# Four accumulators in the first down matmul of a pooled-attention and gated-MLP kernel on one Trainium2 core

## The chip, the cores and the metric

The kernel runs on one core of one Trainium2 chip. The metric is the device time in microseconds (us); three runs of the kernel before gave a median of 284.59 us (284.47 to 284.63). Engines are named as in the profile: PE is TensorE's matmul, PEld its weight load, DVE is VectorE, ACT is ScalarE, POOL is GpSimd, SP is SyncE, which here only issues DMA.

## The reference

Eight batches with eight heads of 576 rows of 64 are attended to keys and values that are averaged over groups of eight rows, so each head has only 72 keys. The result, read as 4608 tokens of 512, goes through an MLP whose activation is `h * cos(h)`.

```python
k_p = k.reshape(B, H, Sp, 8, D).mean(axis=3)       # Sp = 72
v_p = v.reshape(B, H, Sp, 8, D).mean(axis=3)
scores = scale * np.matmul(q, k_p.transpose(0, 1, 3, 2))
attn = softmax(scores)
x = np.matmul(attn, v_p).transpose(0, 2, 1, 3).reshape(4608, 512)
h = x @ w_in                                       # 512 x 2048
out = (h * np.cos(h)) @ w_out                      # 2048 x 512
```

## The kernel before

The tokens are cut into nine tiles of 512 (`t` = 0 to 8). For each tile an up stage multiplies by `w_in` (`up_mm`, L354), takes the cosine on ACT (L364) and the product on DVE (L368), which gives `g_sb`; a down stage then multiplies `g_sb` by `w_out`. While the down stage of tile t runs, the attention of batch b = t + 1 is computed in between, since the next up stage needs it. The order of the work on each engine is the order of the program text; the queues are not reordered.

From tile 1 on the down stage uses seven products in place of eight, for which sums of the blocks of `w_out` are needed. `put_weights(i, nc.vector, ks)` makes them on DVE (L388): for each half `i` four sums named 1, 3, 2 and 4, of which 2 needs 3 and 4 needs 2. Half 0 reads the blocks `w_out_sb[0]` and `[2]`, half 1 the blocks `[1]` and `[3]`. The blocks are loaded in the order 0, 2, 1, 3.

Tile 0 is the only one whose down stage is the plain product, 64 matmuls of 128x128 weights by 512 columns (`down_mm`, L371): four row blocks of 128 tokens (`ms`) times sixteen steps of the contraction (`fc`), four to a block of `w_out` (`cg`). Before, it works on two row blocks at a time, accumulated in `obanks[0]` and `obanks[1]`, and takes for each pair all four blocks of `w_out` in the order 0, 2, 1, 3. `down_out` copies a finished row block to SBUF on DVE (L376) and stores it from SP (L380).

The list `fill` puts the attention of batch 1 between these matmuls: `(n, f)` runs `f` ahead of matmul `n`. `S_(j, bank)` is the scores of unit `j`: four matmuls on 64 rows (L234) and an Exp on ACT (L241). `V_(j, bank)` is the values: four matmuls (L269), two Ln (L275) and an Exp (L276) on ACT, and two multiplies on DVE (L280), which read the same PSUM and write `xT`, the input of the next up stage. With `later` as the last argument the two multiplies are kept back, and `later.pop()()` issues them. `REST` is the last 64 rows of batch 0. `pool_v_mm` pools the values of batch 1 by matmul (L186, with its copy on DVE L188).

PSUM is laid out as three pairs of banks, `banks[0]` to `banks[2]`, and two single ones, `obanks`. The first up stage after tile 0 begins by writing `banks[0]`, then `banks[2]`, then `banks[1]`, then `obanks`.

GpSimd pools the keys and values of batches 2 to 7 (`pool_first`, L157; `pool_rest`, L163 to L169), starting when the keys of batch 2 have landed, during tile 0's down stage. At the very start the keys of batch 0 are pooled by matmul and copied to `kk` by `put_kk`, four copies for each pair of heads (L151).

Of the kernel before, what the change touches and what calls it, by code (L numbers as in the profile page):

```python
# [9 lines left out]
FP32 = mybir.dt.float32  # L10
# [10 lines left out]
def kernel(  # L21
# [9 lines left out]
    nc = tc.nc  # L31
    B, H, S, D = q.shape
    Sp = S // POOL
    d_model = H * D
# [112 lines left out]
    def put_kk(b, ps, pj0, pj1, copy):  # L147
        for a in range(2):
            for r in range(2):
                j = key_slot(b, 2 * pj0 + a, r)  # L150
                copy(out=kk[b % 2][half[r], j:j + pj1 - pj0, 0:Sp], in_=ps[half[a]])  # L151

    def pool_first(b, which):

# [16 lines left out]
    def pool_k_mm(b, bank, pj0, pj1):  # L171

        kb = staged["k", b]
        ps = bank[:, 0:(pj1 - pj0) * Sp].rearrange("p (j n) -> p j n", n=Sp)
        for pj in range(pj0, pj1):
            for t in range(ROW):
                for rows in half:
                    nc.tensor.matmul(ps[rows, pj - pj0, :], lhsT=kb[rows, pj, t, :], rhs=groups[rows, t, :],  # L178
                                     start=(t == 0), stop=(t == ROW - 1))
        return lambda copy: put_kk(b, ps, pj0, pj1, copy)  # L180
# [42 lines left out]
    def scores(b, u, pair):  # L223
        scores_mm(b, u, pair)
        scores_exp(b, u, pair)
# [145 lines left out]
        nc.tensor.matmul(o, lhsT=g_sb[:, fc, ms * 128:(ms + 1) * 128],  # L371
                         rhs=w_out_sb[fc // 4][:, fc % 4, :], start=(fc == 0), stop=(fc == FFCH - 1))

    def down_out(t, ms, ps):
        o = msb.tile([128, 2, d_model], FP32, name="o_two", tag="o_two", bufs=2)[:, 0]
        nc.vector.tensor_copy(out=o, in_=ps)  # L376
        rows_of = out.rearrange("(b p t) m -> b t p m", b=B, t=ROW)
        for i, rows in enumerate(half):
            b_, pos = divmod((t * TILE + ms * 128) // 64 + i, ROW)
            nc.sync.dma_start(out=rows_of[b_, ORDER[pos]], in_=o[rows])  # L380
# [151 lines left out]
    early_inverses += ["p1_sb", "v_sb", "q_sb"] * 3  # L532

    warm_up(10, obanks[0])
    pool_k_mm(0, obanks[1], 0, 2)(vec)
    warm_up(2, banks[1][:, 0, :])
    puts = q_transpose_mm(0, banks[2][:, 0, :], 0, 5), q_transpose_mm(0, obanks[0], 5, 9)
    puts[0](vec)
# [24 lines left out]
    for t in range(NT):  # L563
        b = t + 1
        if t > 0:

            for fp in up_order(t)[0:2]:
                up_mm(t, fp, 0, 2)
        for n, fp in enumerate(up_order(t)):
            up_mm(t, fp, 2 if n < 2 else 0)  # L570
            between = ()
            if t == 0:
                if fp == 4:
                    puts = pool_k_mm(1, obanks[0], 0, 2), pool_k_mm(1, obanks[1], 2, 4)
                elif fp in (5, 6):
                    g0 = 9 * (fp - 5)
                    puts = q_transpose_mm(1, obanks[0], g0, g0 + 5), q_transpose_mm(1, obanks[1], g0 + 5, g0 + 9)
                if fp in (4, 5, 6):
                    puts[0](vec)
                    between = ((puts[1], act),)  # L580
            up_g(t, fp, between)

            late = {5: (1,), 6: (3,)} if t == 1 else {4: (1, 2), 5: (3,)}
            sums = {} if t == 0 else late if b < B else {3: (1, 2), 4: (3,), 5: (4,)}
            put_gs(*[(i, 0) for i in sums.get(n, ())])
            if 0 < t and b < B:
                if n == 0:
                    q_transpose(b)
                    k_transpose(b)
                elif n == 2:  # L590
                    pool_rest(b, "v")
                    if b + 1 < B:
                        nc.gpsimd.tensor_copy(out=gate, in_=kk[b % 2][0:1, H - 1, 0:1])
                        load_q(b + 1)
                        load_kv(b + 1, "v", v)
            if n == 2:
                while stores:
                    stores.pop(0)()
        mms = [(ms, fc) for ms in range(4) for fc in range(FFCH)]
        if t == 0:  # L600
            mms = [(ms, fc) for hm in range(2) for cg in (0, 2, 1, 3) for ms in range(2 * hm, 2 * hm + 2)
                   for fc in range(4 * cg, 4 * cg + 4)]


        def S_(n, bank):
            return lambda: scores(b, us[n], banks[bank])

        later = []

        def V_(n, bank, wait=None):  # L610
            return lambda: values(b, us[n], banks[bank], wait)

        fill = []
        if t < B:
            exp_tables()
            fill = [(1, lambda: scores(t, REST, banks[2])), (16, lambda: values(t, REST, banks[1]))]
        if t == 0:
            fill = [(2, lambda: scores(t, REST, banks[1])), (2, S_(0, 0)), (8, lambda: pool_v_mm(1, banks[2])),
                    (8, lambda: values(t, REST, banks[1])),
                    (8, lambda: put_weights(0, nc.vector, (3, 2))), (8, S_(1, 0)), (8, V_(0, 2)),  # L620
                    (18, S_(2, 1)), (18, lambda: put_weights(0, nc.vector, (4,))),
                    (18, lambda: put_weights(1, nc.vector, (1,))), (21, V_(1, 0, later)), (26, S_(3, 2)), (32, lambda: later.pop()()),
                    (32, V_(2, 1)), (40, V_(3, 0))]
        if t == FIRST:
            early_inverses.clear()
        if t < FIRST:
            fi = 0
            for n, (ms, fc) in enumerate(mms):
                while fi < len(fill) and fill[fi][0] <= n:
                    fill[fi][1]()  # L630
                    fi += 1
                down_mm(obanks[ms % 2], ms, fc)
                if fc == FFCH - 1:
                    down_out(t, ms, obanks[ms % 2])
                if n == 4:
                    put_weights(0, nc.vector, (1,))
                elif n == 36:
                    put_weights(1, nc.vector, (3,))
            put_weights(1, nc.vector, (2, 4))
        else:  # L640
            products, reads = down_products(t)

            def product(i, j=0, k=2 * HF):
                for mm in products[i][j:k]:
                    mm()

            later = []

            u0, u1, u2, u3 = [(b, CHUNKS[i], banks[j]) for i, j in enumerate((2, 1, 0, 1))]
            ur = (t, REST, banks[2])  # L650

            def scores_of(*parts):
                for part in parts:
                    scores_mm(*part)
                for part in parts:
                    scores_exp(*part)

            def muls():
                while later:
                    later.pop(0)()  # L660

            steady, rest = b < B, t < B
            if rest:
                exp_tables()

            product(0, 0, 12)
            product(1, 0, 4)
            product(0, 12)
            reads[0]()
            if steady:  # L670
                scores_of(u0, u1, u2)
            elif rest:
                scores_of(ur)
            product(1, 4)
            if t == 1:
                put_g(2, 0)
            put_gs((1, 1), (2, 1))
            if not steady:
                reads[1]()
            put_gs((3, 1), (4, 1))  # L680
            if steady:
                reads[1]()
                put_g(4, 0)
                values_rows(*u0)
            product(2)
            reads[2]()
            if steady:
                values_rows(*u1)
                values_rows(*u2)
            product(3)  # L690
            reads[3]()
            muls()
            product(4)
            reads[4]()
            muls()
            if steady:
                scores_of(ur, u3)

            product(5, 0, 6)
            if rest:  # L700
                values(*ur, later)
            product(5, 6, 12)
            muls()
            if steady:
                values_rows(*u3)
            product(5, 12)
            reads[5]()
            muls()
            product(6)
            reads[6]()  # L710
        if t < B:
            sin_tables()
        if b + 1 < B:
            if t == 0:
                load_kv(b + 1, "k", k)
                load_q(b + 1)
                load_kv(b + 1, "v", v)
            else:

                nc.gpsimd.tensor_copy(out=gate, in_=g4[0:1, 0, 0:1])  # L720
            pool_first(b + 1, "k")
            if t != 1 and b + 2 < B:
                load_kv(b + 2, "k", k)
            pool_rest(b + 1, "k")
            if t == 1:
                load_kv(b + 2, "k", k)
            pool_first(b + 1, "v")
# [28 lines left out]
```

## Time and profile before

| | |
|---|---|
| median of three runs | 284.59 us |
| span of the profiled execution | 282.8 us |
| tile 0, first down matmul starts | 33.45 us |
| tile 1, first up matmul starts | 53.05 us |
| GpSimd's first pooling of keys starts | 46.37 us |
| down matmul L371, mean of one | 379 ns |
| weight sums L388 at 39.76, 40.48, 43.08 and 43.69 us | 0.68 to 0.69 us each |
| weight sums L388 at 49.00, 53.86 and 55.56 us | 1.30, 1.67 and 1.64 us |
| issue to landing of a block of w_out | 18.2 to 18.7 us |

All times are counted from the start of the span. [...]

### The profile page before, as it was taken

How to read it: one execution, taken by the hardware profiler on the slowest of the kernel's cores; microseconds unless marked ns; L12 is line 12 of the kernel's file. 1: busy time of each engine (PE TensorE's matmuls, PEld its weight loads, DVE VectorE, ACT ScalarE, POOL GpSimd, SP SyncE). 2: the span in 40 equal slices, each digit the busy share in tenths (PEclk: the TensorE clock that was granted, in tenths of full speed). 3: DMA queues.
4: the chain of work that ended last, by engine and by line, in shares of the span. 5: the costliest groups of instructions: out<-in, count | busy, mean ns of one | idle time of the engine just before them, and what ended most of it. 6: DMA issues, size and time to landing. Idle time of an engine off the chain costs nothing.

```text
span 282.8 us, 5887 instructions
## 1 busy us (share of the span) xinstructions
PE 275.2 (97%) x2378; PEld 185.4 (66%) x2378; DVE 212.6 (75%) x313; ACT 167.3 (59%) x199; POOL 132.1 (47%) x146
## 2 busy tenths in 40 slices
PE   7899999999999999999999999999999999999994
PEld 3555554456875687568756975688558855875683
DVE  5448769889946995699568966896689669846972
ACT  3787798368357735774567556655666555436600
POOL 8542114995599259934993389539910000000000
PEclk9999999999999999999999999999999999999999
DMA  7999999795739798997688959882660260005015
GB/s 153 201 206 209 212 207 216 132 190 84 118 60 163 125 215 140 136 175 155 101 148 146 189 80 163 156 174 52 125 148 3 58 148 19 2 21 127 2 37 112
DMA packets 56202, 36.13 MB, mean 128 GB/s; under 512 B 35440, under 2 KB 51312, under 8 KB 56176
## 3 DMA queue, kind: packets, MB, share of 16 engines
q0 software_dynamic: 18208, 18.07, 40.8%
q1 hardware_dynamic: 37328, 17.18, 29.7%
q10 hardware_dynamic: 640, 0.52, 0.8%
q8 instruction: 18, 0.29, 0.4%
q14 instruction: 8, 0.07, 0.1%
HBM read 36.70 MB, written 9.44 MB: 163 GB/s over the span
## 4 chain that ended last, share of the span: by engine, by line
PE 92%; ACT 3%; DMA 2%; DVE 1%; issue 1%; POOL 0%; POOLq 0%; DVEq 0%
PE bank L354 39%; PE obank L432 33%; PE obank L354 5%; PE obank L371 4%; PE bank L234 3%; DMA q_b<-in_q_dram 2%; PE bank L296 2%; PE bank L432 2%; ACT ex L241 1%; PE bank L269 1%; PE obank L178 0%; DVE g_sb L368 0%; PE obank L215 0%; PE bank L186 0%; ACT cos L364 0%
## 5 line engine op out<-in xcount | busy, mean ns | idle before, releaser
L354 PE MATMUL bank<-xT,w_in_sb 128*128 128x512 bf16 x512 | 113.8, 379 | 0.1
L364 ACT ACTIVATE cos<-bank,half_pi 128x1024 f32<-128x1024 f32 x64 | 70.4, 1115 | 55.9 <-PE bank L354 55.9
L354 PEld LDWEIGHTS <-w_in_sb 128*128 128x128 bf16 x576 | 64.9, 113 | 57.4 <-issue 0.3
L368 DVE TENSOR_TENSOR g_sb<-bank,cos 128x1024 bf16<-128x1024 f32 x64 | 77.0, 1221 | 30.5 <-ACT cos L364 30.3
L157 POOL TENSOR_TENSOR half_sums<-kv_st 72x512 f32<-72x512 bf16 x48 | 54.4, 1158 | 8.4 <-DMA kv_st<-in_k_dram 8.0
L241 ACT ACTIVATE ex<-bank 72x1024 bf16<-72x1024 f32 (+1 forms) x40 | 35.0, 931 | 30.0 <-PE bank L234 30.0
L432 PEld LDWEIGHTS <-g 128*128 128x128 bf16 x512 | 47.8, 98 | 5.8
L432 PE MATMUL obank<-w,g 128*128 128x256 bf16 x368 | 42.6, 272 | 0.0
L432 PEld LDWEIGHTS <-g_sb 128*128 128x128 bf16 x384 | 37.0, 98 | 6.4
L163 POOL TENSOR_TENSOR half_sums<-half_sums 72x512 f32<-72x512 f32 x24 | 30.0, 1273 | 0.0
L432 PE MATMUL obank<-w_out_sb,g_sb 128*128 128x256 bf16 x240 | 28.9, 273 | 0.0
L398 DVE TENSOR_TENSOR g<-g_sb 128x1024 bf16<-128x1024 bf16 x32 | 21.9, 685 | 0.3
L720 POOL COPY gate<-g 1x1 bf16<-1x1 bf16 x5 | 0.9, 180 | 37.9 <-DVE inv_rows L299 37.9
L280 DVE TENSOR_TENSOR xT<-bank,inv 64x256 bf16<-64x256 f32 x14 | 5.9, 422 | 15.4 <-ACT inv L276 15.4
L301 DVE TENSOR_TENSOR x_rows<-bank,inv_rows 128x512 bf16<-128x512 f32 x24 | 16.6, 692 | 0.8
L432 PE MATMUL obank<-w_out_sb,g 128*128 128x256 bf16 x112 | 15.6, 273 | 0.0
L432 PE MATMUL obank<-w,g_sb 128*128 128x256 bf16 x128 | 15.3, 272 | 0.0
L371 PE MATMUL obank<-w_out_sb,g_sb 128*128 128x512 bf16 x64 | 15.2, 379 | 0.0
L354 PE MATMUL obank<-xT,w_in_sb 128*128 128x512 bf16 x64 | 15.1, 379 | 0.0
L234 PE MATMUL bank<-qT,kk 64*72 64x128 bf16 (+2 forms) x288 | 12.3, 221 | 0.1
L332 ACT ACT_TABLE_LOAD x9 | 11.5, 1283 | 0.9 <-PEq L740 0.7
L234 PEld LDWEIGHTS <-kk 64*72 64x72 bf16 x288 | 8.7, 110 | 5.1 <-issue 3.4
(99 smaller groups left out, 270.0 us busy)
## 6 DMA issues: line engine op xcount, KB each, us to landing
out_dram<-o_two SPq DMA_DIRECT2D x64, 128.0 KB, 2.4
kv_st<-in_v_dram POOLq DMA_DIRECT2D x8, 576.0 KB, 12.3
kv_st<-in_k_dram POOLq DMA_DIRECT2D x7, 576.0 KB, 8.1
q_b<-in_q_dram POOLq DMA_DIRECT2D x6, 576.0 KB, 7.6
w_in_sb<-in_moe_w_in_dram POOLq DMA_DIRECT2D x4, 512.0 KB, 13.5
w_out_sb<-in_moe_w_out_dram POOLq DMA_DIRECT2D x4, 512.0 KB, 18.6
q_b<-in_q_dram POOLq DMA_DIRECT2D x4, 288.0 KB, 12.3
g_sb<-in_k_dram SPq DMA_DIRECT2D x1, 576.0 KB, 3.4
```

The costliest lines, as they stand in the source:

```text
L157: nc.gpsimd.tensor_tensor(out=s[:, h:h + 2], in0=x[:, h:h + 2, 0:4, :], in1=x[:, h:h + 2, 4:8, :], op=ADD)
L163: add(out=s[:, h:h + 4, 0:2, :], in0=s[:, h:h + 4, 0:2, :], in1=s[:, h:h + 4, 2:4, :], op=ADD)
L234: nc.tensor.matmul(pair[:Sp, bank, c:c + n].rearrange("p (g n) -> p g n", n=64), lhsT=kk[b % 2][half[r], key_slot(b, h0 + i, r), 0:Sp], rh ...
L241: nc.scalar.activation(out=ex[:, 0:nh * n].rearrange("p (a n) -> p a n", a=2), in_=pair[:Sp, :, 0:nh * n // 2], func=ACTF.Exp, scale=scale ...
L301: nc.vector.tensor_tensor(out=x[0:n].rearrange("p (j a d) -> p j a d", j=KCH, a=2), in0=ps[0:n, :, 0:2 * (D + 2)].rearrange("p j (a w) -> ...
L332: nc.scalar.preload_act_table_set("natural_log_exp_and_others")
L354: nc.tensor.matmul(h[j] if h is obanks else h[:, j, :], lhsT=w_in_sb[fc // 4][:, ki, fc % 4:512:4], rhs=xT[:, ki, t * TILE:(t + 1) * TILE] ...
L364: nc.scalar.activation(out=c, in_=ps, func=ACTF.Sin, bias=half_pi[:, :1])
L368: nc.vector.tensor_mul(out=o, in0=ps, in1=c)
L371: nc.tensor.matmul(o, lhsT=g_sb[:, fc, ms * 128:(ms + 1) * 128], rhs=w_out_sb[fc // 4][:, fc % 4, :], start=(fc == 0), stop=(fc == FFCH - 1))
L398: nc.vector.tensor_tensor(out=out[:, f0:f1], in0=x, in1=y, op=op)
L432: mms.append(lambda bank=bank, first=first, g=g, w=w, fc=fc, p=p: nc.tensor.matmul(bank[p], lhsT=g(fc, p), rhs=w(fc), start=(first and fc ...
```

## The change

The plain down stage of tile 0 gets four accumulators: the two `obanks` and the two halves of `banks[1]`. All four row blocks first use the blocks 0 and 2 of `w_out`, and after matmul 31 the blocks 1 and 3, in the row order 2, 3, 0, 1; so the blocks are used as they land. Row blocks 2 and 3 are copied out together, when the second of them is done. As `banks[1]` is taken from matmul 16 on, the attention's units are moved between `banks[0]` and `banks[2]` and to other places in the list, and the multiplies kept back are those of `V_3` in place of `V_1`. The sums 3 and 2 of half 1 are made ahead of matmul 34, before GpSimd's pooling; before, sum 3 came after matmul 36 and sum 2 at the end. The output tiles are allocated as two whole ones in place of four halves. And at the start half of the first pooled-key copies goes to ACT.

```diff
-                copy(out=kk[b % 2][half[r], j:j + pj1 - pj0, 0:Sp], in_=ps[half[a]])
+                (copy if callable(copy) else copy[a])(out=kk[b % 2][half[r], j:j + pj1 - pj0, 0:Sp], in_=ps[half[a]])
...
-    pool_k_mm(0, obanks[1], 0, 2)(vec)
+    pool_k_mm(0, obanks[1], 0, 2)((vec, act))
...
-            mms = [(ms, fc) for hm in range(2) for cg in (0, 2, 1, 3) for ms in range(2 * hm, 2 * hm + 2)
-                   for fc in range(4 * cg, 4 * cg + 4)]
-            fill = [(2, lambda: scores(t, REST, banks[1])), (2, S_(0, 0)), (8, lambda: pool_v_mm(1, banks[2])),
-                    (8, lambda: values(t, REST, banks[1])),
-                    (8, lambda: put_weights(0, nc.vector, (3, 2))), (8, S_(1, 0)), (8, V_(0, 2)),
-                    (18, S_(2, 1)), (18, lambda: put_weights(0, nc.vector, (4,))),
-                    (18, lambda: put_weights(1, nc.vector, (1,))), (21, V_(1, 0, later)), (26, S_(3, 2)), (32, lambda: later.pop()()),
-                    (32, V_(2, 1)), (40, V_(3, 0))]
...
-                down_mm(obanks[ms % 2], ms, fc)
-                if fc == FFCH - 1:
-                    down_out(t, ms, obanks[ms % 2])
-                if n == 4:
-                    put_weights(0, nc.vector, (1,))
-                elif n == 36:
-                    put_weights(1, nc.vector, (3,))
-            put_weights(1, nc.vector, (2, 4))
+            mms = [(ms, 4 * cg + f) for cgs, mss in (((0, 2), (0, 1)), ((0, 2), (2, 3)), ((1, 3), (2, 3, 0, 1)))
+                   for cg in cgs for ms in mss for f in range(4)]
+            acc = [*obanks, banks[1][:, 0, :], banks[1][:, 1, :]]
+            os = [msb.tile([128, 2, d_model], FP32, name="o_two", tag="o_two", bufs=2) for _ in range(2)]
+            fill = [(2, lambda: scores(t, REST, banks[1])), (2, S_(0, 0)),
+                    (4, lambda: put_weights(0, nc.vector, (1,))),
+                    (8, lambda: pool_v_mm(1, banks[2])), (8, lambda: values(t, REST, banks[1])),
+                    (8, lambda: put_weights(0, nc.vector, (3, 2))), (8, S_(1, 0)), (8, V_(0, 2)),
+                    (18, lambda: put_weights(0, nc.vector, (4,))), (20, lambda: put_weights(1, nc.vector, (1,))),
+                    (20, V_(1, 0)), (28, S_(2, 2)), (34, lambda: put_weights(1, nc.vector, (3, 2))), (35, S_(3, 0)), (36, V_(2, 2)),
+                    (44, V_(3, 0, later)), (57, lambda: later.pop()())]
...
+                down_mm(acc[ms], ms, fc)
+                if fc == FFCH - 1 and ms != 2:
+                    for m in (2, 3) if ms == 3 else (ms,):
+                        down_out(t, m, acc[m], os[m // 2][:, m % 2])
+            put_weights(1, nc.vector, (4,))
```

## The prediction before the run

> **What bounds the kernel now.** I read the page's busy shares first, then the chain that ended last in order of time, then the timelines of PE and of DVE from 40 us on, where the edited stage lies. The page:
>
> ```profile
> PE 275.2 (97%) x2378; PEld 185.4 (66%) x2378; DVE 212.6 (75%) x313; ACT 167.3 (59%) x199; POOL 132.1 (47%) x146
> PEclk9999999999999999999999999999999999999999
> ```
>
> TensorE is busy 97% at full clock, so a change can help only where PE stands still, and hurts wherever it makes PE stand still. Is there standing still in the first down stage (33.45 to 53.05 us)? The chain, in order of time (start, length, what):
>
> ```profile
> 38.70 2.16 PE obank L371 x10
> ...
> 45.66 1.73 PE obank L371 x8
> 47.38 0.04 issue
> 47.42 0.61 PE bank L269 x4
> 48.03 5.18 PE obank L371 x24
> 53.22 5.18 PE bank L354 x24
> 58.40 1.73 PE obank L354 x8
> 60.12 6.91 PE bank L354 x32
> ```
>
> From 38 us to the end nearly everything is PE, and from 48 us on no wait is left. So what the stage gains or loses goes one to one into the total. The PE timeline of the stage:
>
> ```profile
> 40.79 0.41 PE L234 MATMUL bank<-qT,kk 64*72 64x256 bf16 x4
> 41.13 0.82 PE L371 MATMUL obank<-w_out_sb,g_sb 128*128 128x512 bf16 x3
> 41.79 0.60 PE L269 MATMUL bank<-ex,vz 72*128 72x256 bf16 x4
> 42.23 1.24 PE L371 MATMUL obank<-w_out_sb,g_sb 128*128 128x512 bf16 x5
> 45.49 1.89 PE L371 MATMUL obank<-w_out_sb,g_sb 128*128 128x512 bf16 x8
> 47.42 0.61 PE L269 MATMUL bank<-ex,vz 72*128 72x256 bf16 x4
> ```
>
> A row's length holds the drain of its last matmul; starts give the pace: 24 matmuls in 5.18 us is 0.216 us each. The eight from 45.49 are issued by 47.22, and the next group starts at 47.42: 0.20 us of real waiting. Now DVE:
>
> ```profile
> 41.66 1.39 DVE L280 TENSOR_TENSOR xT<-bank,q_sb 64x512 bf16<-64x512 f32 x2 [0.48 <-ACT q_sb L276]
> 43.08 0.69 DVE L388 TENSOR_TENSOR w<-w_out_sb,w 128x1024 bf16<-128x1024 bf16 x1
> 43.69 0.68 DVE L388 TENSOR_TENSOR w<-w_out_sb 128x1024 bf16<-128x1024 bf16 x1
> 45.98 1.39 DVE L280 TENSOR_TENSOR xT<-bank,p_sb 64x512 bf16<-64x512 f32 x2
> 49.00 1.30 DVE L388 TENSOR_TENSOR w<-w_out_sb,w_out_sb 128x1024 bf16<-128x1024 bf16 x1
> 52.39 0.69 DVE L376 COPY o_two<-obank 128x512 f32<-128x512 f32 x1 [0.67 <-PE obank L371]
> 53.26 0.69 DVE L376 COPY o_two<-obank 128x512 f32<-128x512 f32 x1 [0.17 <-PE obank L371]
> 53.86 1.67 DVE L388 TENSOR_TENSOR w<-w,w_out_sb 128x1024 bf16<-128x1024 bf16 x1
> ```
>
> The pair of multiplies from 45.98 ends at 47.37; PE's group at 47.42 writes the same bank pair (banks[0]), so that wait is for them. Its first matmul writes only the first bank of the pair, which only the first multiply (done at about 46.67) reads, yet it waited for the second. **The wait is for the pair of banks as a whole.** Much hangs on this below.
>
> **What the Trainium skill says.** "PSUM — Partial Sum Buffer", PSUM bank collisions raise a hardware error: a bank must be guarded by bank and quadrant. That would let PE into one bank while DVE reads its neighbour; the 47.42 start shows the program waiting more coarsely. "SBUF — State Buffer", Who interferes with whom: a DVE instruction with two SBUF inputs contends with a GpSimd one that reads SBUF. The trace agrees: weight sums take 0.69 us before GpSimd's pooling starts (46.37) and 1.30 to 1.67 after. "TensorEngine Tiling (Array Packing)", Key Properties: changing the tiling mode drains TensorE. Trace: from the last of three L371 matmuls to L269 the step is 0.21 us, but a score group (64 rows) begins 0.31 us after the last L371 start and the next L371 0.34 us after the group, about 0.09 us lost each way. The change keeps the number of such switches.
>
> **The change part by part.** I number the 64 down matmuls n.
>
> Start-up: half of the first pooled-key copies moves to ACT. The four DVE copies run from 6.71 to 7.99, but the next chain piece waits for q's DMA to 7.65 and then for its transposes, and DVE takes up qT only at 8.19. ACT is idle from 5.4 to 8.4. Cost and gain: nothing, hidden by that DMA.
>
> n = 0 to 17: same order, same fills, so PE reaches n=8 at 38.54 as before. Blocks 1 and 3 of w_out move from n=16 and 24 to n=32 and 48. They were issued at 21.30 and 24.12 and take 18.6 us, so they land at 39.9 and 42.7 or a little earlier; n=16 ran at 40.27 and n=24 at 42.88. PE did not wait for them; the later use gains nothing.
>
> n = 18 to 34, PE: n=8 to 19 without a score group, 12 x 0.216, so V_1 (values, L269) at 41.13; 0.44 for it, n=20 at 41.57; eight more to 43.30; S_2 (scores, L234) at 43.39, n=28 at 43.73; n=34 at 45.04; ready for S_3 at about 45.35.
> DVE in the same time: V_0's multiplies end 43.05 as before; sum 4 of half 0 to 43.77, sum 1 of half 1 to 44.37 (both as before); then V_1's two multiplies, 1.39, 44.41 to 45.80. Their input is in time (ACT: V_1's two Ln from 41.77, 1.20, and Exp 0.63, done 43.6).
> S_3 writes banks[0], which V_1's multiplies read until 45.80, so it starts at 45.85. **New wait: 0.50 us.** In place of it the old 0.20 wait disappears.
>
> n = 35 to 63, PE: n=35 at 46.19, V_2 at 46.42, n=36 at 46.86, V_3 at 48.59, n=44 at 49.03, n=55 from 51.40 to 51.78, n=63 done issuing at 53.34 (0.30 later than 53.05).
> The two weight sums at n=34 go in DVE at 45.83 to 47.9 (0.69, then about 1.3 under pooling; 1.67 at worst) while V_2 waits for ACT anyway: after Exp of S_3 (46.30 to 47.30) its Ln and Exp end at 49.16, its multiplies at 50.57. That removes 1.3 + 1.67 us of slow sums, but DVE had 20.4 us busy in 25 there and PE never waited for them: no gain.
>
> The end: the outputs of row blocks 2 and 3 now lie in the two halves of banks[1] and are both copied after n=55; then come V_3's multiplies, held back until n=57. DVE is in order, so: copy 2, copy 3, multiply, multiply. If the copy of block 2 waits for the last write of the bank pair, which is how I read 47.42, it starts at 51.81; two copies 1.41, two multiplies 1.42: done 54.64. The next up stage begins with banks[0], which V_3's multiplies read: its first matmul at about 54.70 instead of 53.34. **New wait: 1.36 us.** Behind it in PE's queue stands the whole rest of the kernel. In the old kernel these multiplies were over at 51.72.
>
> Sum: 0.50 - 0.20 + 1.36 = 1.66 us, 284.59 + 1.66 = 286.2. Nothing later takes it back, since PE has no wait from 48 us on. DVE afterwards: copies of blocks 0 and 1 to 56.1, one slow sum to 57.8, and the first product of the up stage, at 57.13 before and 1.66 later now, is hardly touched. The stores of tile 0 come about 2 us later in SP's queue, ahead of the transposes that the scores at 69.14 need; these transposes were issued by 63.70, so over 3 us of slack remain.
>
> **The rivals.**
> Waits by bank, not by pair: the copy of block 2 starts after n=51 (50.95), block 3's at 51.81, multiplies end at 53.92; up starts at 53.98 (+0.93), or, if the first up matmuls need only the first multiply, only a second short wait of 0.2 remains (+0.5). 285.1 to 285.5. For it: the rule by bank and quadrant; against it: 47.42.
> No new waits (multiplies early enough, by an order of work that I misjudge): the 0.20 goes, 284.4, not slower. Against: three DVE durations added in program order.
> Faster by 0.2% would need 0.57 us. Such a sum is not there: all gaps of the stage beyond the mode switches are some 0.6 us, most of them ahead of n=8 where nothing changes. Only if the real reason for the block order, landing w_out blocks, bit in unprofiled runs could it come; the profiled run took 284.58, the median, so no. About 284.0.
> Worse: pooling also slows the weight sums and delays V_2's multiplies past 50.9: 286.6 or more.
>
> **How the numbers follow.** Pair-wise waits 0.74 (286.2, spread 285.9 to 286.6), by bank 0.12, no new waits 0.09, faster 0.05. Range 285.0 to 286.6. Slower by over 0.2% (285.16): 0.85, the by-bank case lying across the edge; same 0.10; faster 0.05.
>
> **What would show it.** In the new profile: a PE wait on DVE L280 of about 0.5 us before the score group near 45.8; two L376 copies back to back near 51.8 and then L280 twice; PE's first L354 of tile 1 near 54.7 with L280 as its releaser; from there on the old chain, shifted. Wrong would be a PE without gaps from 41 to 53, copies that start before n=55 has ended, or an up stage that starts before V_3's multiplies end.

## The result and the profile after

The changed kernel takes 286.59 us in the median of six runs (286.13 to 287.19) against 284.53 for six runs of the kernel before (the three runs above and three more): a ratio of 1.0078, 95% interval 1.0061 to 1.0094. It is slower by 2.06 us between the medians and by 2.2 us by the ratio, where 1.66 was forecast; on the 284.59 us from which the forecast started, the ratio makes 286.8. From the page of the changed kernel, the busy times and the shares of the chain that ended last:

```profile
PE 273.9 (96%) x2356; PEld 185.3 (65%) x2378; DVE 210.5 (74%) x311; ACT 167.9 (59%) x201; POOL 132.0 (46%) x146
...
PE 89%; ACT 3%; DVE 3%; DMA 2%; issue 1%; POOL 0%; POOLq 0%; DVEq 0%
```

The shares of the chain before were:

```profile
PE 92%; ACT 3%; DMA 2%; DVE 1%; issue 1%; POOL 0%; POOLq 0%; DVEq 0%
```

PE's share falls from 92% to 89% and DVE's rises from 1% to 3%. (22 matmul records are missing from this trace: PE has 2356 where PEld has 2378.) In order of time, the chain of the changed kernel in the down stage (start, length, what):

```profile
44.12 0.68 DVE xT L280
44.82 0.71 DVE xT L280
45.52 0.04 issue
45.56 0.41 PE bank L234 x4
...
51.53 1.29 DVE o_two L375 x2
52.82 0.03 issue
52.85 0.68 DVE xT L280
53.54 0.01 issue
53.55 0.70 DVE xT L280
54.26 0.05 issue
54.30 5.37 PE bank L354 x24
```

Where the kernel before had PE from 48.03 us on without a break, DVE now stands in the chain twice: V_1's multiplies ahead of the score group S_3, and the two copies with V_3's multiplies ahead of tile 1's up stage. The PE timeline gives the size of the waits:

```profile
43.47 1.68 PE L371 MATMUL bank<-w_out_sb,g_sb 128*128 128x512 bf16 x7
45.56 0.41 PE L234 MATMUL bank<-qT,kk 64*72 64x256 bf16 x4 [0.41 <-DVE xT L280]
...
51.33 1.89 PE L371 MATMUL obank<-w_out_sb,g_sb 128*128 128x512 bf16 x8
54.30 0.41 PE L354 MATMUL bank<-xT,w_in_sb 128*128 128x512 bf16 x1 [1.08 <-DVE xT L280]
```

Counted by starts, at 0.216 us a matmul, the seven from 43.47 are issued by 44.98, and with 0.09 for the switch to 64 rows S_3 could begin at 45.07: 0.49 us of waiting. The eight from 51.33 are issued by 53.06 and the up stage begins at 54.30: 1.24 us. (A down matmul's record is 379 ns long, while the next one starts after 216 ns. The bracket counts from the end of the last record and so shows less.) And DVE in the changed kernel:

```profile
44.12 1.39 DVE L280 TENSOR_TENSOR xT<-bank,p_sb 64x512 bf16<-64x512 f32 x2
45.54 0.69 DVE L387 TENSOR_TENSOR w<-w_out_sb,w_out_sb 128x1024 bf16<-128x1024 bf16 x1
46.27 1.52 DVE L387 TENSOR_TENSOR w<-w,w_out_sb 128x1024 bf16<-128x1024 bf16 x1
48.95 1.39 DVE L280 TENSOR_TENSOR xT<-bank,v_sb 64x512 bf16<-64x512 f32 x2 [1.15 <-ACT v_sb L276]
51.53 1.29 DVE L375 COPY o_two<-bank 128x512 f32<-128x512 f32 x2 [1.20 <-PE bank L371]
52.85 1.39 DVE L280 TENSOR_TENSOR xT<-bank,q_sb 64x512 bf16<-64x512 f32 x2
```

DVE idles 1.20 us before the copies although row block 2 was complete about 0.86 us (four matmuls) earlier than block 3: the first copy, too, waited for the last write to the pair of banks.

From the first down matmul to the first up matmul of tile 1 the stage takes 19.60 us before (33.45 to 53.05) and 21.12 after (33.18 to 54.30): 1.52 us of the loss. From there to DVE's last addition the two kernels agree to 0.03 us (226.08 and 226.11). What is left is at the very end: the span ends 3.68 us after that addition before, and 4.36 us after it now. The prediction had put nothing outside the stage. (The two profiled spans, 282.8 and 284.8 us, differ by 1.95 and not by the 2.2 of these parts, because the down stage of the second also began 0.27 us earlier.)

### The profile page after: what moved, and what is told of

It is laid out like the page before. It is cut to its first block, busy times and chain, and to the rows that moved or that the text cites. A ratio compares the mean times of both kernels' runs of the same rounds, so it can differ in the third digit from the quotient of the medians.

```text
span 284.8 us, 5864 instructions
## 1 busy us (share of the span) xinstructions
PE 273.9 (96%) x2356; PEld 185.3 (65%) x2378; DVE 210.5 (74%) x311; ACT 167.9 (59%) x201; POOL 132.0 (46%) x146
## 4 chain that ended last, share of the span: by engine, by line
PE 89%; ACT 3%; DVE 3%; DMA 2%; issue 1%; POOL 0%; POOLq 0%; DVEq 0%
PE bank L354 39%; PE obank L431 33%; PE obank L354 5%; PE bank L234 3%; DMA q_b<-in_q_dram 2%; PE bank L296 2%; PE bank L431 2%; ACT ex L241 1%; DVE xT L280 1%; PE bank L269 1%; PE bank L371 1%; PE bank L186 1%; PE obank L371 1%; DVE w L387 0%; DVE o_two L375 0%
```

## The experiments

Two theories to begin with. A: two waits of PE for DVE make the loss in the stage. B: part of the loss comes from elsewhere, from ACT's stream, which got two more instructions. The waits of the stage can be taken away one at a time by the order of DVE's work alone. Every kernel was timed in five rounds beside the kernel before, whose medians were 284.68 us in the first four comparisons and 284.61 in the last four. "Stage" below is the stretch from the first down matmul to the first up matmul of tile 1, "tail" that from the end of DVE's last addition to the end of the span, each in the profiled execution.

**V_3's multiplies not kept back.**

```diff
-                    (44, V_(3, 0, later)), (57, lambda: later.pop()())]
+                    (44, V_(3, 0))]
```

> The changed kernel, but V_3's two multiplies are issued at matmul 44 and not held back to 57. Theory A (two DVE waits of PE make up the loss in the stage): Exp of V_3 ends at 50.8 in the changed kernel, so the multiplies run 50.8 to 52.2, ahead of the two copies; the first L354 of tile 1 then finds banks[0] free and starts when PE is ready, about 53.1 in place of 54.3. Total down by 1.2 us, 285.4. Rival B (the loss sits in the start or the tail of the kernel, for instance in the ACT stream with its two more copies): total stays within 0.3 us of 286.6. Rival C (the copies of the bank pair would then block PE in turn): no more than half of 1.2 us is gained and PE waits for L375.

Measured: 285.36 us, ratio to the kernel before 1.0032 (1.0018 to 1.0047). Stage 19.89 us, so 1.23 less than in the changed kernel, tail 4.22. This profiled execution began its down stage late, at 35.09 us; its DVE timeline shows the order that matters:

```profile
52.75 1.39 DVE L280 TENSOR_TENSOR xT<-bank,q_sb 64x512 bf16<-64x512 f32 x2 [0.49 <-ACT q_sb L276]
54.17 1.29 DVE L375 COPY o_two<-bank 128x512 f32<-128x512 f32 x2
```

The multiplies end at 54.14, the up stage starts at 54.98 behind PE's own work, and its chain there holds nothing but PE. The copies of the bank pair, now last, block nothing, as tile 1 writes that pair only 16 matmuls later. Theory A holds for the larger wait. Rival C falls, and so does B, which had the total unmoved.

**V_1's multiplies ahead of the two weight sums.**

```diff
-                    (18, lambda: put_weights(0, nc.vector, (4,))), (20, lambda: put_weights(1, nc.vector, (1,))),
-                    (20, V_(1, 0)), (28, S_(2, 2)),
+                    (20, V_(1, 0)), (20, lambda: put_weights(0, nc.vector, (4,))),
+                    (20, lambda: put_weights(1, nc.vector, (1,))), (28, S_(2, 2)),
```

> The changed kernel, but the two weight sums that stand ahead of V_1's multiplies in DVE's queue are put behind them. Theory A: Exp of V_1 ends at 43.4, the multiplies run 43.4 to 44.8 instead of 44.1 to 45.5, and S_3 starts without a wait, 0.5 us earlier; the wait at the end of the stage stays (1.2 us). Total 286.1. Rival B: no difference to 286.6. Rival C (the sums, now later, meet GpSimd's pooling from 45.8 on, run at 1.1 to 1.6 us each and push V_2's multiplies back): less than 0.2 us gained, with a later start of the two copies.

Measured: 286.14 us, ratio 1.0051 (1.0031 to 1.0071). Stage 20.64 us, 0.48 less than in the changed kernel. DVE:

```profile
43.98 1.39 DVE L280 TENSOR_TENSOR xT<-bank,p_sb 64x512 bf16<-64x512 f32 x2 [0.61 <-ACT p_sb L276]
45.41 0.69 DVE L387 TENSOR_TENSOR w<-w_out_sb,w 128x1024 bf16<-128x1024 bf16 x1
46.02 0.68 DVE L387 TENSOR_TENSOR w<-w_out_sb 128x1024 bf16<-128x1024 bf16 x1
46.62 1.64 DVE L387 TENSOR_TENSOR w<-w_out_sb,w_out_sb 128x1024 bf16<-128x1024 bf16 x1
48.30 1.53 DVE L387 TENSOR_TENSOR w<-w,w_out_sb 128x1024 bf16<-128x1024 bf16 x1
49.85 1.39 DVE L280 TENSOR_TENSOR xT<-bank,v_sb 64x512 bf16<-64x512 f32 x2
51.64 1.29 DVE L375 COPY o_two<-bank 128x512 f32<-128x512 f32 x2 [0.40 <-PE bank L371]
```

S_3 no longer waits. The two sums that were moved still take 0.69 and 0.68 us; it is the sum behind them that now meets GpSimd's pooling (from 46.27 us in this run) and takes 1.64 us in place of 0.69, and V_2's multiplies start later. So rival C's slow sum appears, one place further back; but the copies still wait for PE (0.40 us idle), so that costs nothing, and the stage gains what theory A said. (By the times alone the intervals of the two kernels overlap.)

**The first key copies all on DVE again, in the changed kernel.**

```diff
-    pool_k_mm(0, obanks[1], 0, 2)((vec, act))
+    pool_k_mm(0, obanks[1], 0, 2)(vec)
```

> The changed kernel without the half of the first pooled-key copies on ACT: all four copies on DVE again. The changed kernel's span ends 4.36 us after DVE's last addition, the kernel before's 3.68 us after it; that 0.7 us is the part of the loss that lies outside the stage. Theory A: that difference has nothing to do with the split, total 286.6 within 0.2 us. Rival B (two more instructions on ACT shift its stream, and the last stores that ACT issues come later): tail back to 3.7 us, total 286.0.

Measured: 286.37 us, ratio 1.0054 (1.0032 to 1.0075). Stage 21.12 us as in the changed kernel, tail 3.76 in place of 4.36. The gain is 0.22 us between the medians and 0.7 by the ratios, and the intervals overlap, so the time alone decides nothing; the tail speaks for B.

**The split alone, in the kernel before.**

```diff
-                copy(out=kk[b % 2][half[r], j:j + pj1 - pj0, 0:Sp], in_=ps[half[a]])
+                (copy if callable(copy) else copy[a])(out=kk[b % 2][half[r], j:j + pj1 - pj0, 0:Sp], in_=ps[half[a]])
...
-    pool_k_mm(0, obanks[1], 0, 2)(vec)
+    pool_k_mm(0, obanks[1], 0, 2)((vec, act))
```

> The kernel before with that split alone. Theory A: 284.6 within 0.2 us, since q's DMA and its transposes end after the copies in any case. Rival B: tail of 4.4 us after DVE's last addition, total 285.2.

Measured: 285.03 us, ratio 1.0008 (0.9997 to 1.0020). By time it can't be told from no change. Stage 19.61, tail 4.13 in place of 3.68. So the profiles so far fall into two groups by the split: 3.68 and 3.76 without, 4.02 (V_1 first), 4.13, 4.22 and 4.36 with it. In the timelines the two last stores that ACT issues, as one row, show where the tail begins to grow. The kernel before:

```profile
278.50 1.19 SPq L468 DMA_DIRECT2D out_dram<-o_two  x2
278.70 0.42 DVE L448 TENSOR_TENSOR o_two<-obank,p_sb 128x256 f32<-128x256 f32 x1 [0.45 <-PE obank L432]
278.80 1.21 ACTq L468 DMA_DIRECT2D out_dram<-o_two  x2
```

The changed kernel:

```profile
279.78 1.19 SPq L467 DMA_DIRECT2D out_dram<-o_two  x2
279.98 0.42 DVE L447 TENSOR_TENSOR o_two<-obank,p_sb 128x256 f32<-128x256 f32 x1 [0.45 <-PE obank L431]
280.05 1.42 ACTq L467 DMA_DIRECT2D out_dram<-o_two  x2
```

SP's pair takes 1.19 us in both, ACT's 1.21 and 1.42: the last store begins 0.60 us after DVE's last addition has ended, in place of 0.32, although ACT's store before it ends 0.22 to 0.23 us after the addition in both. All four kernels with the split so far have it at 0.60 or 0.61 and both without at 0.30 to 0.32.

This start is 0.28 of the 0.68 us. The other 0.40 lies in the transfer: from start to landing ACT's last store takes 2.06 us before and 2.45 in the changed kernel. SP's last store, which starts 0.03 us after the addition in both, lands 2.01 us after its start before and 2.84 now.

The moved copies are 270 us away. Is it them, or only the number of ACT's instructions?

**Two one-element copies on ACT, in the kernel before.** The key copies stay on DVE.

```diff
+    tiny = consts.tile([1, 1], FP32, name="tiny")
...
+        if t in (3,):
+            for _ in range(2):
+                nc.scalar.copy(out=tiny, in_=half_pi[0:1, 0:1])
         if t < B:
             sin_tables()
```

> The kernel before, plus two one-element copies on ACT near the end of tile 3's down stage, where ACT is idle; no key copy is moved. If the longer tail of the split comes from the number of ACT's instructions (where a fetch of its program falls), the last store that ACT issues begins 0.60 us after DVE's last addition ends in place of 0.30, the tail is 4.0 to 4.4 us and the total 285.0. If it comes from the key copies themselves, or from chance, the store begins at 0.30, the tail stays 3.7 and the total 284.7.

Measured: 285.55 us, ratio 1.0041 (1.0024 to 1.0057). Stage 19.61, tail 4.29; the last store begins at 0.58. Two copies of a single element, in the middle of the kernel, lengthen its end as the split does. The timeline:

```profile
278.49 0.42 DVE L448 TENSOR_TENSOR o_two<-obank,p_sb 128x256 f32<-128x256 f32 x1 [0.45 <-PE obank L432]
278.57 1.40 ACTq L468 DMA_DIRECT2D out_dram<-o_two  x2
```

**The split and ten one-element copies, in the kernel before.** The key copies are split as in the change, and the loop above runs with two copies in each of the tiles 2 to 6 (the two diffs above, with this one line in place of the one that names tile 3).

```diff
+        if t in (2, 3, 4, 5, 6):
```

> The kernel before with the split of the first key copies, plus ten one-element copies on ACT, two near the end of each of the down stages of tiles 2 to 6. If it is where a fetch falls that counts, twelve more instructions put it ahead of the last stores, where ACT waits for DVE in any case: last store of ACT at 0.30 us after DVE's last addition, tail 3.7, total 284.7. If every ACT instruction more makes the tail longer: 0.6 us or later, tail over 4.1, total 285.0 or more.

Measured: 284.58 us, ratio 1.0002 (0.9993 to 1.0011). Stage 19.61, tail 3.62, last store at 0.31:

```profile
279.08 0.42 DVE L448 TENSOR_TENSOR o_two<-obank,p_sb 128x256 f32<-128x256 f32 x1 [0.45 <-PE obank L432]
279.16 1.21 ACTq L468 DMA_DIRECT2D out_dram<-o_two  x2
```

With twelve more instructions the tail does not grow, where with two it grew by 0.45 us (the split) and 0.61 us (the tiny copies). So it is neither the moved copies by themselves nor the amount of ACT's work. What fits is the place at which some boundary in ACT's stream falls: this run's expectation was built on that and came true, but no trace shows the boundary itself.

**Row block 2 copied as soon as it is done, in the changed kernel.**

```diff
-                if fc == FFCH - 1 and ms != 2:
-                    for m in (2, 3) if ms == 3 else (ms,):
-                        down_out(t, m, acc[m], os[m // 2][:, m % 2])
+                if fc == FFCH - 1:
+                    down_out(t, ms, acc[ms], os[ms // 2][:, ms % 2])
```

> The changed kernel, but row block 2 is copied out as soon as its last matmul is done (after matmul 51) and not together with block 3. If the program waits for the pair of banks as a whole: matmul 52, which writes the other bank of the pair, waits for that copy, about 0.8 us of PE standing still, then about 0.6 us at the next up stage: total 286.7. If it waits by bank: no wait at matmul 52, and the up stage waits only about 0.6 us: 286.0.

Measured: 286.81 us, ratio 1.0074 (1.0060 to 1.0089). Stage 21.47 us, 0.35 longer than in the changed kernel. PE:

```profile
51.32 1.02 PE L371 MATMUL bank<-w_out_sb,g_sb 128*128 128x512 bf16 x4 [0.78 <-DVE o_two L375]
52.18 1.89 PE L371 MATMUL obank<-w_out_sb,g_sb 128*128 128x512 bf16 x8
54.55 0.62 PE L354 MATMUL bank<-xT,w_in_sb 128*128 128x512 bf16 x2 [0.48 <-DVE xT L280]
```

The four matmuls of block 3 write one bank while DVE copies out of the other bank of the pair, and wait for it. The pair is waited for as a whole, as the prediction read it from the 47.42 start.

**All three costs taken out of the changed kernel.** The first three edits together.

> The changed kernel with all three of its costs taken out: V_3's multiplies at matmul 44, V_1's multiplies ahead of the two weight sums, and all first key copies on DVE. Theory A+B (two waits in the stage, and the ACT stream's tail): 286.6 - 1.2 - 0.5 - 0.3 = 284.6, within 0.3 us of the kernel before, no wait of PE on DVE L280 between 41 and 55 us, tail 3.7 us after DVE's last addition. Rival C (the four-accumulator order costs something by itself): 285.0 or more. Rival D (the block order and the early sums do gain, hidden so far by the waits): 284.2 or less.

Measured: 284.17 us, ratio to the kernel before 0.9983 (0.9970 to 0.9996): faster than the kernel before by some 0.5 us, with an interval of 0.1 to 0.85. Stage 19.40 us, which is 21.12 less 1.23 and 0.48 to 0.01 us, and 0.20 less than before; tail 3.76. Its chain in order of time:

```profile
44.85 0.34 PE bank L234 x4
45.19 0.32 PE bank L371
45.51 0.44 PE bank L269 x4
...
50.71 1.73 PE obank L371 x8
52.43 5.18 PE bank L354 x24
57.61 1.73 PE obank L354 x8
```

No wait for DVE is left between 41 and 55 us. Rival C falls: the four accumulators cost nothing by themselves. The total is where rival D had put it and a little below the 0.3 us that A and B allowed, but the interval is too wide to choose between them. The stage shows a gain of 0.20 us, which is the wait at 47.42 of the kernel before, and no more; so no gain from the order of the blocks or from the early sums appears in it.

## Why the prediction was right in the stage and wrong outside it

The bound: right. What PE loses in the stage reaches the end unchanged, 1.52 us at tile 1's start and 1.55 at DVE's last addition, both counted from the start of the down stage.

The wait for V_1's multiplies: forecast 0.50, measured 0.49; taking it away gave 0.48.

The wait at the end of the stage: forecast 1.36, measured 1.24; taking it away gave 1.23. The order was as forecast, copies after matmul 55, then the multiplies; two copies back to back took 1.29 us where 1.41 was added up. The reading that waits are for the pair of banks, on which 0.7 us of the forecast hung, was tested by itself and holds. So the rival by bank is out for this program.

The wait that disappears, 0.20 us: right, and it is all that the stage gains.

Weight sums ahead of the pooling, no gain: right for this stage. Sum 2 of half 1 came at 46.27, after pooling had begun at 45.80, and took 1.52 us, so only sum 3, begun just before it, escaped; and when two other sums were put between V_1's multiplies and these, so that both ran slowly, PE lost nothing.

The failed step is the first one, the start-up: "Cost and gain: nothing, hidden by that DMA." It put the two instructions that ACT gets at no cost. At the start no effect shows: the first transposes began anywhere between 6.76 and 8.04 us in ten profiles, with the split between 7.26 and 8.04, without it between 6.76 and 7.70. The split could hardly have gained there, for a reason that the step didn't see. The key copies before and in the changed kernel:

```profile
6.71 1.28 DVE L151 CAST kk<-obank 64x144 bf16<-64x144 f32 x4 [1.86 <-PE obank L178]
```

```profile
6.66 0.63 DVE L151 CAST kk<-obank 64x144 bf16<-64x144 f32 x2 [1.81 <-PE obank L178]
7.39 0.56 ACT L151 CAST kk<-obank 64x144 bf16<-64x144 f32 x2 [1.78 <-DVE kk L151]
```

ACT's two copies wait for DVE's two, in all six kernels with the split, so that here the four end at 7.95 us in place of 7.99.

The cost came at the other end of the kernel. The step looked only at the place of the edit; with two instructions more on ACT the tail grew from 3.68 to 4.36 us. With that the sum is 0.49 + 1.24 - 0.20 + 0.68 = 2.2 us, against 2.06 between the medians and 2.2 by the ratio; without it, 1.5. The range's upper end, 286.6, had no room for a term of this kind, since its bounds came from the stage alone.

The profiles show this term clearly, in ten kernels out of ten; the times support it less well. Taking the split out of the changed kernel gave 0.22 to 0.7 us, and putting it into the kernel before 0.2 to 0.35, with an interval that includes no change. But the stage's 1.5 us lies below the measured interval, 1.7 to 2.7 us (the ratio's, times 284.59), so something outside the stage is needed, and the tail is the only such growth that the two profiles show.

What stays open is what the boundary is. The profile's DMA part for the tail of the changed kernel lists one instruction transfer beside the last stores:

```profile
q10 hardware_dynamic: 171, 0.13, 16.2%
q1 hardware_dynamic: 157, 0.13, 15.9%
q14 instruction: 1, 0.01, 0.5%
```

In the kernel with twelve more instructions there is none in the tail, and in the kernel before it comes after the stores have landed. Over all ten profiles this goes with the tail: in the six kernels with the long one the instruction transfer starts 1.3 to 1.8 us after DVE's last addition, while the last stores are under way; in the four others it starts 2.4 us after the addition or later, when they have landed, or 5.9 us ahead of it. That fits a fetch of ACT's program, moved by two instructions to the last stores. But it is argued: nothing in the profile says whose program it is or shows ACT waiting for it, and in the changed kernel the transfer starts 1.73 us after the addition, when the store that began late, at 0.60, had long been issued. So the store didn't wait for that transfer to arrive, and whether the transfer lengthens the landing of the stores is not shown either. Shown is only the effect of the count. Open too is why two tiny copies cost 0.7 to 1.6 us in time (interval of the ratio) when the tail explains 0.6 of it.

## What to carry to other kernels

When accumulators share an allocation with buffers of another chain, look at what one wait covers: here a read of one bank held back writes to its neighbour, and a multiply that was kept back to let copies through cost 1.23 us because the next stage's first write needed its bank. On a kernel bound by one engine, list for each write to a reused buffer the in-order queue of the engine that frees it, and put first what that engine must do for the bound one. Here a change of an instruction count far from the end moved the end by half a microsecond: compare the tails before giving a difference of that size to the stage that was edited.

## What the runs showed of the hardware that was not expected

The end of the kernel moved with the number of ACT's instructions: the last store of ACT began 0.58 to 0.61 us after DVE's last addition with two instructions more, and 0.30 to 0.32 with none or twelve more, it took 2.11 to 2.45 us from start to landing against 2.02 to 2.06, and the tails were 4.02 to 4.36 against 3.62 to 3.76 us. The start varied from profile to profile: the first transposes, which wait for q's DMA, began between 6.76 and 8.04 us, and the first down matmul between 32.87 and 35.09.
